# One core, linear attention into a two-layer network: the order of 4920 planned operations searched anew

## The chip, the cores and the metric

The program runs on one core of a Trainium2 chip. The metric is the device time of one execution in microseconds (us). TensorE multiplies matrices, VectorE, ScalarE and GpSimd (POOL) do the elementwise work, SP issues the DMAs. Each engine runs its own queue strictly in the order in which the program was written, and waits on semaphores for the others.

## The reference

```python
# attention: batch 8, heads 8, 576 tokens, head width 64, 128 random features
def phi(x):                                   # x already scaled by 64 ** -0.25
    h = einsum('bhsd,md->bhsm', x, omega) - sum(x * x, -1) / 2
    return exp(h - max(h, -1)) / sqrt(m)
kv, z = einsum('bhsm,bhsd->bhmd', phi(k), v), sum(phi(k), 2)
attn  = einsum('bhsm,bhmd->bhsd', phi(q), kv) / (einsum('bhsm,bhm->bhs', phi(q), z) + 1e-6)
# network over x = attn as 4608 tokens x 512
out = gelu(x @ w_in) @ w_out                  # w_in 512 x 2048, w_out 2048 x 512, gelu by erf
```

## The kernel before

The work is cut into operations of some 0.1 to 3 us: a Python function that issues a few instructions on one engine. There are 4920 of them. They are first recorded, each with what it reads and writes, and then issued one by one in the order of a table of numbers, ORDER, written out at the top of the file. The table sets the order of every engine's queue, SP's among them. A letter behind a number chooses one of three rings of PSUM banks. The loop that walks the table refuses an order in which an operation stands ahead of one that it depends on, and does nothing else:

```python
for x in ORDER.split():
    i = x.rstrip('abc')
    o, pick = self.ops[int(i)], x[len(i):] or 'a' * 4
    assert o.deps <= done and o.after <= done
    ...
    put(o)          # issues the operation's instructions
    done.add(o)
```

**Attention** is done in 32 units (u0 to u31), each two heads of one batch. Units 0 to 7 are plain (fp32): TensorE multiplies the features (pair, shared, L658, L665), VectorE takes the maximum of each tile (top, L670), ScalarE the exponential (exp_tiles, L674, in units 0 to 3; from unit 4 on VectorE shifts and one exps, L683, does the whole unit), TensorE sums keys by values (kv, L690), transposes the queries (q_trans, L728) and multiplies the two (num_plain, L738). Then ScalarE copies the denominator out (den), VectorE inverts it (rcp) and divides (div). Units 8 to 31 split operands in high and low parts. Their operations, as far as they are named below: x_high (ScalarE, L868) and x_low (POOL, L877) split the input, proj (TensorE, L885) and proj_q (L907) multiply the features, proj_add (VectorE, L895) adds and takes maxima, q_blocks (L910, L912), q_shift (L936), q_back (L943) and q_low (L949) on VectorE prepare the queries, k_shift (POOL, L903) shifts the keys, k_high (POOL, L408) and k_low (VectorE, L978) split them, kv_split (TensorE, L989) and kv_d (VectorE, L1010) form the sums, num (TensorE, L747) the result; v_max and v_b (VectorE, L1013, L970) scale the values.

**Weights.** 16 pieces are loaded (w_load, L475) and unpacked: w_hi (ScalarE, L480), w_shift (VectorE, L491), w_round (POOL, L497).

**The network** runs over 13 blocks of tokens: 256, 256, ten of 384, 256. In blocks 1 to 8, mm1(n,c) (TensorE, L1176) multiplies chunk c of the hidden layer in three parts of four matmuls into a PSUM bank of a ring of two, gelu and g_high (ScalarE, L1184, L1188) and g_low (VectorE, L1192) turn it into operands, and mm2 (TensorE, L1200 to L1202, three matmuls) multiplies by w_out. So mm1(n,c) can't begin before g_low(n,c-2) has left the bank. Block 0 runs in fp32 (L1171, L1197). Blocks 9 to 12 do the first product in seven products of half blocks (w_prod, L1389; w_mm2, L1487 to L1489; b_low and others); the sums of weights that they need are made by s_sum2 and s_sum (POOL, L1308 to L1317, L1301) and s_low (VectorE, L1327). An operation warm (TensorE, L434) multiplies zeros 22 times; nobody uses its result.

The order mixes all of this: while TensorE multiplies one block, the attention units of later batches pass through the other engines.

Of the kernel before, what the change touches and what calls it, by code (L numbers as in the profile page):

```python
# [34 lines left out]
0 3 6 7 151 42 41 157 4 1 8 43 9bca 14b 2 76 15 12 16 10 152 13 17 154 153 11 18 44aba 20 155 19 49b 45 21 47 50 51 163 77  # L35
156 52cc 158 27 55 22ba 48 160 53 159 5 54 161 56 31 46 23 29c 169 111 112 78 28 79cba 30 165 32 162 62 164 82 33cb 80 83
64b 166 57 34 167 81 35 65 36 84b 170 175 649 85 66b 113 58 114cba 86 172 63 171 119 115 87 117 116 173 120 90 121 37cc 24
59 67 25 91 60 92 88 181 650 38 89 39 177 176 68bb 40 93 122cc 69 178 118 70 97 179 652 98 71 168 99b 653 101b 72ba 26 123
100 187 651 685 94 655 102 127ba 125 656 182 654 73 184 657 183 103ab 74 124 185 658 75 104 659 126 105 193 188 189 132ba
128 660 106 174 190 136b 663 134 191 133 661 137 107bc 664 135 662 665 199 192 687 686 138cb 95 108 666 194 109 195 196  # L40
110 139 197 180 140 186 141 671 667 61 673 205 723 201 129 198 142bb 200 292 672 130 96 248 150 674 131 202 293 143 294
# [1581 lines left out]
```

## Time and profile before

| | |
|---|---|
| median of 3 runs | 970.92 us (970.18 to 971.43) |
| the profiled execution, first to last instruction | 968.7 us |
| TensorE busy | 945.4 us, 98% |
| VectorE busy | 768.5 us, 79% |
| ScalarE busy | 754.1 us, 78% |
| POOL busy | 416.9 us, 43% |
| mean granted clock of TensorE | 0.996 |
| moved by DMA | 71.0 MB, 73 GB/s |

The profile is of one execution; its span is 2.2 us below the median of the runs, which have some time around the first and last instruction. A busy TensorE is not one at its peak: the matmuls overlap, and each record lasts until its result is out. In the rows PE is TensorE, PEld its weight loads, DVE VectorE, ACT ScalarE; L12 is line 12 of the kernel before.

### The profile page before, as it was taken

How to read it: one execution, taken by the hardware profiler on the slowest of the kernel's cores; microseconds unless marked ns; L12 is line 12 of the kernel's file. 1: busy time of each engine (PE TensorE's matmuls, PEld its weight loads, DVE VectorE, ACT ScalarE, POOL GpSimd, SP SyncE). 2: the span in 40 equal slices, each digit the busy share in tenths (PEclk: the TensorE clock that was granted, in tenths of full speed). 3: DMA queues.
4: the chain of work that ended last, by engine and by line, in shares of the span. 5: the costliest groups of instructions: out<-in, count | busy, mean ns of one | idle time of the engine just before them, and what ended most of it. 6: DMA issues, size and time to landing. Idle time of an engine off the chain costs nothing.

```text
span 968.7 us, 18815 instructions
## 1 busy us (share of the span) xinstructions
PE 945.4 (98%) x6572; PEld 623.6 (64%) x6572; DVE 768.5 (79%) x2008; ACT 754.1 (78%) x1583; POOL 416.9 (43%) x620
## 2 busy tenths in 40 slices
PE   6989999999999999999999999999999999999998
PEld 5756666655556556566665666666657677677677
DVE  3889889999989988999997998999888764662322
ACT  6998688998798988988899788988887765664443
POOL 3464316784658526555553553542553302030000
PEclk9999999999999999999999999999999999999999
DMA  8985124421123123123222222221121000000000
GB/s 261 265 264 168 48 53 125 113 85 38 51 61 98 42 83 86 39 64 104 80 63 71 64 64 68 53 76 48 38 61 53 19 1 34 2 12 23 1 34 23
DMA packets 46286, 71.01 MB, mean 73 GB/s; under 512 B 13680, under 2 KB 22256, under 8 KB 46192
## 3 DMA queue, kind: packets, MB, share of 16 engines
q1 hardware_dynamic: 46192, 69.81, 25.0%
q8 instruction: 52, 0.85, 0.4%
q14 instruction: 42, 0.34, 0.1%
HBM read 60.36 MB, written 9.44 MB: 72 GB/s over the span
## 4 chain that ended last, share of the span: by engine, by line
PE 80%; DVE 10%; ACT 5%; issue 2%; DMA 2%; POOL 1%; SPq 0%; ACTq 0%; POOLq 0%; DVEq 0%
PE h L1176 20%; PE acc L1200 6%; PE acc L1201 6%; PE acc L1202 6%; PE at L1389 6%; PE h L1389 5%; PE acc L1487 4%; PE acc L1488 4%; PE acc L1489 4%; PE at L747 3%; PE acc L1197 3%; PE h L1171 3%; PE at L907 2%; PE at L885 2%; PE at L989 2%
## 5 line engine op out<-in xcount | busy, mean ns | idle before, releaser
L877 POOL TENSOR_TENSOR r<-xt,r 64x256 fp32r<-64x256 f32 (+2 forms) x216 | 176.9, 829 | 187.3 <-ACT r L868 160.1
L1176 PE MATMUL h<-xh,wih 128*128 128x384 f16 (+1 forms) x512 | 163.7, 320 | 4.2 <-DVE gl L1192 4.0
L1176 PE MATMUL h<-xh,wil 128*128 128x384 f16 (+1 forms) x512 | 163.7, 320 | 0.0
L1176 PE MATMUL h<-xl,wih 128*128 128x384 f16 (+1 forms) x512 | 163.7, 320 | 0.0
L1200 PE MATMUL acc<-woh,gh 128*128 128x512 f16 x368 | 140.4, 381 | 0.0
L1202 PE MATMUL acc<-wol,gh 128*128 128x512 f16 x368 | 139.5, 379 | 0.0
L1201 PE MATMUL acc<-woh,gl 128*128 128x512 f16 x368 | 139.4, 379 | 0.0
L1176 PEld LDWEIGHTS <-wih 128*128 128x128 f16 x1024 | 98.0, 98 | 61.0 <-issue 0.9
L868 ACT CAST r<-xt 128x256 fp32r<-128x256 f32 (+2 forms) x216 | 83.6, 404 | 17.1 <-PE at L907 9.8
L1192 DVE SCALAR_TENSOR_TENSOR gl<-h,bs,gh 128x384 f16<-128x384 f32 (+1 forms) x128 | 75.8, 592 | 10.1 <-ACT gh L1188 8.6
L1184 ACT ACTIVATE h<-h,bs 128x384 f32<-128x384 f32 (+1 forms) x128 | 69.1, 539 | 15.4 <-PE h L1176 14.5
L1188 ACT ACTIVATE gh<-h,bs 128x384 f16<-128x384 f32 (+1 forms) x128 | 72.3, 565 | 9.9 <-PE acc L1202 7.4
L1176 PEld LDWEIGHTS <-wil 128*128 128x128 f16 x512 | 50.0, 98 | 36.9 <-issue 7.2
L1487 PE MATMUL acc<-woh,gh 128*128 128x512 f16 (+1 forms) x192 | 69.5, 362 | 0.0
L1489 PE MATMUL acc<-wol,gh 128*128 128x512 f16 (+1 forms) x192 | 69.4, 361 | 0.0
L1488 PE MATMUL acc<-woh,gl 128*128 128x512 f16 (+1 forms) x192 | 69.4, 361 | 0.0
L1389 PEld LDWEIGHTS <-w 128*128 128x128 f16 x768 | 59.8, 98 | 7.0
L1202 PEld LDWEIGHTS <-gh 128*128 128x128 f16 x368 | 36.0, 98 | 43.4
L885 PE MATMUL at<-om,r 128*128 128x256 f32 x216 | 58.3, 351 | 1.3 <-DVE mx L918 0.7
L758 ACT ACTIVATE dt<-at,vsc 64x288 f32<-64x288 f32 x96 | 47.6, 496 | 10.7 <-PE at L747 8.4
L1200 PEld LDWEIGHTS <-gh 128*128 128x128 f16 x368 | 35.7, 97 | 28.5
L907 PE MATMUL at<-r,om 128*128 128x288 f32 x192 | 50.7, 355 | 1.1 <-POOL w L1308 0.6
(294 smaller groups left out, 2506.9 us busy)
## 6 DMA issues: line engine op xcount, KB each, us to landing
xt<-in_kT SPq DMA_DIRECT2D x56, 288.0 KB, 4.0
xt<-in_qT SPq DMA_DIRECT2D x56, 288.0 KB, 3.8
out_x<-o SPq DMA_DIRECT2D x35, 256.0 KB, 2.0
raw<-in_w_in SPq DMA_DIRECT2D x16, 512.0 KB, 5.2
raw<-in_w_out SPq DMA_DIRECT2D x16, 512.0 KB, 4.6
w<-in_v SPq DMA_DIRECT2D x24, 320.0 KB, 3.1
vt<-in_v SPq DMA_DIRECT2D x8, 320.0 KB, 6.3
out_x<-o SPq DMA_DIRECT2D x2, 128.0 KB, 1.7
```

Of the source, the lines that this page charges most:

```text
L868: nc.scalar.copy(G['r', u, x][:, 0:b - a], xf[:, a:b])
L877: nc.gpsimd.tensor_tensor(r, xf[D:, a:b], r, op=ALU.subtract)
L885: nc.tensor.matmul(o[:, t], r[:, t * P:(t + 1) * P], om, start=True, stop=True)
L1176: nc.tensor.matmul(h[:, 0:t], w, (G['xh', n, j], G['xh', n, j], G['xl', n, j])[k][:, 0:t], start=(i == 0), stop=(i == 3 * NJ - 1))
L1192: nc.vector.scalar_tensor_tensor(G['gl', n, c][:, 0:t], G['h', n, c][:, 0:t], G['bs', n][:, 3:4], G['gh', n, c][:, 0:t], op0=ALU.mult, op1 ...
L1200: nc.tensor.matmul(acc, gh[:, s], woh[:, c, c0:c1], start=(c == 0), stop=False)
L1201: nc.tensor.matmul(acc, gl[:, s], woh[:, c, c0:c1], start=False, stop=False)
L1202: nc.tensor.matmul(acc, gh[:, s], wol[:, c, c0:c1], start=False, stop=(c == NF - 1))
L1389: nc.tensor.matmul(b[:, g * h:(g + 1) * h], w, x[:, kt], start=first and k == 0, stop=last and k == 6 * GP - 1, skip_group_check=True)
L1487: nc.tensor.matmul(acc, gh, woh[:, c, c0:c1], start=begin, stop=False)
L1488: nc.tensor.matmul(acc, gl, woh[:, c, c0:c1], start=False, stop=False)
L1489: nc.tensor.matmul(acc, gh, wol[:, c, c0:c1], start=False, stop=end)
```

## The change

The table ORDER is replaced; nothing else in the file differs. The table is said to come from a new search, with durations read from a trace of these very operations. It has 190 lines for the old 196, so that every line of code below it has a number lower by 6. The first line of each:

```diff
 ORDER = """
-0 3 6 7 151 42 41 157 4 1 8 43 9bca 14b 2 76 15 12 16 10 152 13 17 154 153 11 18 44aba 20 155 19 49b 45 21 47 50 51 163 77
+0 3 4 6 9bca 1 10 7 11 14b 151 41 42 15 8 16 12 17bc 13 20 44aaa 152 153 49b 18 45 21 47 19 50 154 157 46 76 27ca 29c 31b 51
...
 """
```

Every engine issues as many instructions as before: TensorE 11194 with weight loads, VectorE 2010, ScalarE 1579, POOL 625, SP 217. Two places of the queues follow.

ScalarE's queue from its first instruction. et and w_71 are the exponentials of unit 0 and unit 1, raw is the raw weight piece, acc, h and at are PSUM banks. Before:

```order
L674 ACT_TABLE_LOAD
L674 ACTIVATE et<-acc,nm 128x128 x2
L480 ACTIVATE raw<-raw 128x1024
L674 ACTIVATE et<-h,nm 128x128 x4
L674 ACTIVATE et<-acc,nm 128x128 x4
L674 ACTIVATE et<-at,nm 128x128 x8
L674 ACTIVATE w_71<-acc,nm 128x128 x2
L504 ACTIVATE w_71,wmax<-w_71 128x1024
```

Now:

```order
L668 ACT_TABLE_LOAD
L668 ACTIVATE et<-acc,nm 128x128 x6
L668 ACTIVATE et<-h,nm 128x128 x4
L474 ACTIVATE raw<-raw 128x1024
L668 ACTIVATE et<-h,nm 128x128 x4
L668 ACTIVATE et<-acc,nm 128x128 x4
L668 ACTIVATE w_71<-at,nm 128x128 x4
L668 ACTIVATE w_71<-acc,nm 128x128 x2
```

Ten exponentials of unit 0 stand ahead of the first w_hi (raw) where two stood, and the first w_abs (L504) has gone further back.

VectorE's queue up to g_low(2,3), the gl in the last row but one before, for which the matmul mm1(2,5) waits. Rows of proj_add (ISA) are left out where they repeat. Before:

```order
L936 TENSOR_TENSOR w32_71<-w32_71,nq_2459 128x1152
L949 TENSOR_TENSOR ql_2505<-qt_2262,qh_2325 128x576
L1010 TENSOR_TENSOR kvl_2513<-kvz_2377,kvh_2497 128x256
L895 ISA et_82,nm_2371<-at_2492,lo_2503 128x128
...
L970 SCALAR_TENSOR_TENSOR vb_1266<-w32_71,vsc_1798,vb_1266 128x10x64
L1327 SCALAR_TENSOR_TENSOR w32_71<-w32_71,wsc_80 128x256
L910 STREAM_TRANSPOSE et_82<-at_2526 128x288
L912 TENSOR_REDUCE mx_2527<-et_82 128x9
L943 STREAM_TRANSPOSE qt_2551<-w32_71 128x576
L1192 SCALAR_TENSOR_TENSOR gl_2559<-h_2402,bs_1464,gh_2546 128x384
L978 TENSOR_TENSOR vt_73<-w32_71,vt_73 128x256 x2
```

Now (g_low(2,3) is the gl of the fourth row):

```order
L889 ISA et_82,nm_2351<-at_2435,lo_2456 128x128
L1321 SCALAR_TENSOR_TENSOR w32_71<-xa_83,wsc_80,w32_71 128x256
L964 SCALAR_TENSOR_TENSOR vb_1246<-w32_71,vsc_1802,vb_1246 128x10x64
L1186 SCALAR_TENSOR_TENSOR gl_2517<-h_2413,bs_1464,gh_2499 128x384
L889 ISA et_82,nm_2351<-at_2439,lo_2491 128x128
...
L943 TENSOR_TENSOR ql_2521<-qt_2367,qh_2424 128x576
L1004 TENSOR_TENSOR kvl_2531<-kvz_2374,kvh_2495 128x256
L930 TENSOR_TENSOR w32_71<-w32_71,nq_2404 128x1152
L904 STREAM_TRANSPOSE et_82<-at_2503 128x288
L906 TENSOR_REDUCE mx_2504<-et_82 128x9
```

The q_shift (w32_71 with nq), both q_low (ql), kv_d (kvl) and the q_blocks stand behind g_low where they stood ahead of it.

## Rows read from the trace of the kernel before

**Rows 1.** The page, part 1: busy time, share of the span, instructions.
```profile
PE 945.4 (98%) x6572; PEld 623.6 (64%) x6572; DVE 768.5 (79%) x2008; ACT 754.1 (78%) x1583; POOL 416.9 (43%) x620
```
**Rows 2.** Busy time by stretch: from:to, length, each engine's us, clock, DMA share, GB/s.
```profile
0.00:75.00 75.00, 62.66 (x497) 46.34 (x498) 51.83 (x134) 62.61 (x148) 36.73 (x36) 0.95 0.86 259
160.00:320.00 160.00, 154.97 (x977) 96.89 (x976) 150.98 (x410) 140.50 (x305) 108.00 (x163) 1.00 0.24 68
725.00:969.00 244.00, 240.39 (x2108) 176.52 (x2105) 121.54 (x272) 138.66 (x281) 37.06 (x62) 1.00 0.06 20
```
**Rows 3.** TensorE's waits, 75 to 960 us: who for whom, total us, times, longest.
```profile
PE h L1176 <- DVE gl L1192: 4.0, 7, 1.3
PE at L989 <- DVE vt L978: 1.0, 1, 1.0
PE at L885 <- DVE mx L918: 0.7, 1, 0.7
PE at L885 <- POOL r L877: 0.6, 1, 0.6
PE at L907 <- POOL w L1308: 0.6, 1, 0.6
PE at L907 <- DVE nm L895: 0.6, 1, 0.6
PE h L1176 <- DVE vexp L1030: 0.2, 1, 0.2
```
**Rows 4.** Timeline of TensorE at a wait: start, us, line, tiles; idle before in brackets.
```profile
217.10 0.38 PE L1201 MATMUL acc<-woh,gl 128*128 128x512 f16 x1
217.31 0.38 PE L1202 MATMUL acc<-wol,gh 128*128 128x512 f16 x1
218.98 0.32 PE L1176 MATMUL h<-xh,wih 128*128 128x384 f16 x1 [1.29 <-DVE gl L1192]
```
**Rows 5.** Timeline of the start: VectorE's maxima, ScalarE, TensorE.
```profile
8.70 0.68 DVE L670 TENSOR_REDUCE nm<-h 128x4 f32<-128x512 f32 x1
...
8.82 0.63 ACT L674 ACTIVATE et<-acc,nm 128x128 f32<-128x128 f32 x2 [6.81 <-DVE nm L670]
10.75 1.17 ACT L480 ACTIVATE raw<-raw 128x1024 f32<-128x1024 f32 x1 [1.30 <-DMA raw<-in_w_in]
11.81 1.13 ACT L674 ACTIVATE et<-h,nm 128x128 f32<-128x128 f32 x4
...
5.19 0.55 PE L658 MATMUL acc<-om,xt 64*128 64x128 f32 x1 [5.19 <-DMA xt<-in_kT]
6.85 0.42 PE L658 MATMUL h<-om,xt 64*128 64x128 f32 x1
8.24 3.39 PE L434 MATMUL h<-w 128*128 128x256 bf16 x22
```
**Rows 6.** Busy time by 5 us (columns as in rows 2), 15 to 25 us.
```profile
15.00:20.00 5.00, 3.27 (x29) 2.67 (x25) 2.54 (x6) 5.00 (x15) 0.14 (x1) 1.00 0.98 237
20.00:25.00 5.00, 3.27 (x21) 2.71 (x22) 0.84 (x5) 5.00 (x17) 3.46 (x2) 0.52 1.02 335
```
**Rows 7.** Groups by line: total us, mean ns of one, idle before.
```profile
L936 DVE TENSOR_TENSOR w<-w,nq 128x1152 f32<-128x1152 f32 x11 | 15.2, 1380 | 2.2 <-POOL nq L930 1.7
L949 DVE TENSOR_TENSOR ql<-qt,qh 128x576 fp32r<-128x576 f32 x48 | 40.2, 838 | 0.4 <-ACT qh L946 0.2
L1327 DVE SCALAR_TENSOR_TENSOR w<-w,wsc 128x256 f16<-128x256 f32 x18 | 12.9, 721 | 0.0
L903 POOL TENSOR_TENSOR et<-et,nm 128x1152 f32<-128x1152 f32 x13 | 28.6, 2197 | 7.5 <-DVE nm L895 7.3
```
**Rows 8.** Timelines of VectorE and POOL ahead of that wait.
```profile
214.53 2.33 DVE L1327 SCALAR_TENSOR_TENSOR w<-w,wsc 128x256 f16<-128x256 f32 x1
213.95 2.62 POOL L903 TENSOR_TENSOR et<-et,nm 128x1152 f32<-128x1152 f32 x1 [1.06 <-DVE nm L895]
```
**Rows 9.** Timeline of TensorE at the last num_plain(u2,1).
```profile
51.10 0.66 PE L738 MATMUL h<-qh,kvz 128*64 128x288 f32 x4
```

More of the change, by code (lines that the diff above doesn't have):

```diff
@@ L34 @@
 ORDER = """
-0 3 6 7 151 42 41 157 4 1 8 43 9bca 14b 2 76 15 12 16 10 152 13 17 154 153 11 18 44aba 20 155 19 49b 45 21 47 50 51 163 77
-156 52cc 158 27 55 22ba 48 160 53 159 5 54 161 56 31 46 23 29c 169 111 112 78 28 79cba 30 165 32 162 62 164 82 33cb 80 83
-64b 166 57 34 167 81 35 65 36 84b 170 175 649 85 66b 113 58 114cba 86 172 63 171 119 115 87 117 116 173 120 90 121 37cc 24
-59 67 25 91 60 92 88 181 650 38 89 39 177 176 68bb 40 93 122cc 69 178 118 70 97 179 652 98 71 168 99b 653 101b 72ba 26 123
@@ L39 @@
-100 187 651 685 94 655 102 127ba 125 656 182 654 73 184 657 183 103ab 74 124 185 658 75 104 659 126 105 193 188 189 132ba
-128 660 106 174 190 136b 663 134 191 133 661 137 107bc 664 135 662 665 199 192 687 686 138cb 95 108 666 194 109 195 196
-110 139 197 180 140 186 141 671 667 61 673 205 723 201 129 198 142bb 200 292 672 130 96 248 150 674 131 202 293 143 294
[153 rows of a table removed]
-4423 4372 3470 3887 3468 4424 4373 4371 4434 3471 3469 4438 4374 4369 3891 3472 4435 4425 3889 4432 4439 4375 3892b 4492
-4433 4442 4491 4376 3894 4377 3893 4378 3896 4379 3895 4436 3900 4497 4437 3897 4498 3905 4451 3901 3898 3909 4452 3906
@@ L197 @@
-4293 3899 3907 4038 3473 4385 3910 3474 4382 3908 3902 4440 3475 4502 4441 4300 3903 4388 3911 3913b 3904 4301 3912 3476
[4 rows of a table removed]
-4466 3977 4467 3978 4468 4395 4469 4479 4470 3979 4396 3950b 4471 4397 3952 4477 3951 3980 4480 3953 3954 4478 4398 3958
-3955 3956 3963 4472 3959 3957 3981 3964 4481 4482 3965 4473 3960 3966 3982 4542 3967 3961 4543 4006 4483 4503 4007 4474
-3962 3968 3983b 4475 3969 4008 3970 4045 4009 3984 4010 3985 3987 3986 3989 3988 3993 4011 3994 4012 4046 3995 4013 4047
-4484 4049 4014 3990 4015 4485 3991 4016 3992 4494 4017 4048 4507 3998 4050 4508 3996 4051 4018 3999 4052 4002 4053 4054
@@ L206 @@
-4057b 4003 3997 4004 4019 4000 4005 4020 4058 4001 4021 4495 4496 4022 4023 4059 4024 4055 4025 4061 4056 4026 4027 4499
-4028 4500 4060 4029 4062 4063 4067 4064 4065 4504 4068 4032 4512 4066 4513 4069 4033 4517 4072 4070 4505 4071 4076 4030
-4589 4501 4073 4031 4506 4080 4518 4077 4078 4103 4074 4079 4104 4034 4075 4509 4519 4081 4035 4105 4510 4521 4514 4106
-4511 4525 4520 4529 4107 4526 4082b 4522 4084 4083 4530 4515 4086 4085 4516 4090 4533 4087 4088 4523 4091 4527 4095 4092
-4528 4108 4089 4096 4109 4524 4097 4099 4098 4486 4100 4531 4110 4487 4532 4111 4488 4112 4534 4113 4489 4114 4138 4093
@@ L211 @@
-4535 4139 4101 4094 4115b 4536 4537 4102 4538 4117b 4116 4539 4540 4140 4118 4119 4541 4141 4120 4121 4142 4143 4122 4125
-4567 4544 4546 4545 4130 4548 4126 4552 4568 4550 4570 4144 4131 4547 4145 4571 4551 4569 4554 4127 4146 4549 4123 4555
-4147 4553 4132 4124 4556 4148 4557 4149 4134 4128 4558 4150 4559 4135 4560 4129 4173 4136 4561 4174 4137 4562 4133 4175
-4564 4151 4563 4176 4565 4573 4566 4581 4582 4152b 4572 4583 4574 4177 4584 4585 4586 4154 4153 4575 4178 4753 4587 4593
-4576 4156 4588 4155 4179 4157 4577 4180 4578 4160 4158 4579 4181 4165 4161 4580 4182 4166 4169 4167 4159 4162 4590 4183
@@ L216 @@
-4168 4170 4184 4591 4594 4185 4163 4592 4186 4754 4164 4171 4607b 4755 4595 4172 4597 4187 4596 4599 4598 4188 4756 4601
-4600 4189 4757 4603 4602 4605 4190 4608 4604 4758 4609b 4606 4611 4610 4759 4191 4613 4612 4192 4193 4614 4194 4615 4195
-4760 4617 4196 4618 4622 4616 4197 4198 4626 4623 4630b 4632 4631 4627 4199 4633 4200 4619 4634 4201 4620 4202 4636 4635
-4621 4640 4637 4638 4645 4641 4761 4653 4646 4649 4628 4647 4629 4654 4624 4639 4665b 4648 4625 4655 4666 4667b 4656 4668
-4669 4650 4671 4670 4675 4672 4642 4657 4676 4658 4659 4680 4684 4660 4661 4662 4663 4664 4688 4643 4689 4685 4644 4673
@@ L221 @@
-4700 4651 4674 4690 4652 4701 4691 4681 4692 4677 4693 4694 4695 4702b 4696 4703 4704 4697 4705 4698 4699 4706 4678 4679
-4710 4707 4708 4723 4711 4686 4715 4709 4682 4687 4724 4683 4725 4719 4726 4720 4727 4716 4717 4728 4762 4729 4712 4763
-4730 4764 4718 4766 4731 4765 4768 4767 4732 4769 4774b 4733 4734 4776b 4713 4735 4721 4714 4736 4777 4722 4737 4775 4738
-4778 4780 4779 4739 4781 4770 4740 4772 4771 4743 4741 4773 4744 4782 4745 4783 4746 4784 4789 4785 4786 4749 4747 4793
-4748 4742 4750 4794 4797 4787 4790 4799b 4788 4798 4820 4795 4800 4796 4801 4791 4821 4792 4751 4802 4803 4752 4807 4804
@@ L226 @@
-4805 4822 4808 4806 4823 4809 4824 4825 4826 4827 4828 4829 4830 4812 4831 4816 4810 4813 4855 4811 4817 4832b 4818 4814
-4819 4856 4815 4833 4857 4858 4859 4834b 4860 4835 4861 4862 4863 4836 4864 4837 4838 4842 4839 4840 4847 4843 4841 4844
-4865 4851 4848 4867 4866 4868 4890 4852 4869b 4871 4870 4845 4891 4872 4853 4846 4873 4849 4854 4877 4850 4874 4875 4892
-4878 4876 4882 4879 4886 4883 4893 4887 4884 4894 4895 4885 4896 4897 4898 4899 4900 4901 4902 4880 4888 4903 4881 4889
-4904 4905 4908 4906 4909 4910 4911 4907 4912 4913 4914 4917 4915 4916 4918 4919
+0 3 4 6 9bca 1 10 7 11 14b 151 41 42 15 8 16 12 17bc 13 20 44aaa 152 153 49b 18 45 21 47 19 50 154 157 46 76 27ca 29c 31b 51
@@ new lines @@
+48 43 22ba 52ab 23 53 77 28 32 79baa 158 155 57ca 30 159 160 54 55 84c 56 24 80 161 156 85 62ba 163 64b 111 169 162 58 164
+112 33ac 86 65 82 166 81 34 25 165 35 36 63 83 66a 59 114bba 119a 67 26 171 78 87aa 115 117 170 167 37cc 120 116 172 68bb 121
+90 38 173 175 649 88 91 176 60 650 39 40 61 181 69 113 92aa 178 89 122cc 93 70 123 97aa 652 71 118 177 655 98 124 99b 653 100
+656 179 101a 654 102 125 187 651 182 72bb 73 103cb 184 74 657 183 126 658 75 686 127aa 659 132ca 136b 104 105 168 188 133 106
@@ new lines @@
+134b 185 137 660 107bc 2 663 135 661 94 662 664 108 174 665 190 193 128 109 129 685 110 194 95 189 130 138bb 721 671 139 191
+96 131 192 196 140 195 673 666 672 674 180 688 186 146 141 199 292 293 142bb 200 197 294 296 295 198 205 297 667 689 723 248
[146 rows of a table added]
+3465 3466 3459 4430 4419 4291 3460 3463 4434 3874 3470 4424 3471 3472 3890a 3467 4368 4428 4361 4435 3883 4431 4425 3867 4292
+4438 4420 4429 3468 3875 4432 3884 3469 4433 3885 4289 3886 3888 3887 4490 4436 3473 3474 3891 3475 3892b 4039 4371 3894 4437
@@ new lines @@
+3893 4439 4366 4369 4492 4290 4442 3476 4491 4364 3895 4440 4441 3896 3897 3900 4443 3901 4298 4365 4444 3905 4367 3477 3889
+4497 3906 3902 3479 3478 4299 4372 4373 4445 3898 4374 3899 3907 4375 4376 4377 3482 3903 3909 4378 4446 3908 3936 3937 3910
+3904 4447 3480 3871 4451 4300 4448 4379 3911 3938 3913b 3939 4036 4301 3912 3914 3915a 4302 3940 3483 4382 3917 3919 3941
+4449 4303 3916 4304 3942 4450 3920 4457 4293 4388 3918 4452 3923 4383 3943 4458 3944 3945 3946 4386 4461 4040 4453 4455 3947
@@ new lines @@
+3924 3921 4462 4305 4380 3925 3922 4306 3926 3928 4307 4387 4389 3971 4459 3932 3972 3948a 3927 3933 3934 4460 4456 4381 4454
+3973 3935 4391 3974 4463 4037 4464 4390 4465 3975 4466 3929 3930 4493 4392 3931 4393 4394 4467 4468 4469 4043 3976 4470 4476
+3977 3978 4479 4395 3979 4044 3950b 3980 4396 3981 4397 4477 3949 3952 4471 3982 3951 4398 4041 3954 4478 4498 3953 4472 3955
+3958 4482 3959 3956 4502 3963 3960 3967 3961 3957 4006 3962 4007 4008 4009 3964 3968 3965 3966 3969 3983b 3970 4010 3984
@@ new lines @@
+3985a 3987 4045 4384 4483 3989 4042 4473 4011 4012 4013 4484 3986 4014 4485 3481 4015 3988 4494 3993 3994 3998 4046 3990 4503
+4002 4047 4016 4048 4507 3999 3991 4000 4057b 4003 3992 4017 4495 3995 4001 4058 4508 4474 4059a 3996 4496 3997 4049 4018
+4019 4050 4060 3484 4004 4005 4020 4051 4061 4499 4504 4021 4022 4480 4023 4062 4500 4063 4053 4064 4024 4055 4065 4026 4512
+4052 4054 4067 4072 4513 4073 4517 4056 4027 4028 4029 4032 4518 4033 4066 4068 4481 4505 4501 4030 4069 4074 4076 4070 4077
@@ new lines @@
+4103 4506 4078 4071 4025 4104 4034 4075 4079 4080a 4509 4510 4081 4519 4514 4511 4105 4521 4106 4107 4082b 4083 4525 4084
+4108 4109 4086 4522 4085 4526 4090 4095 4087 4110 4088 4515 4529 4096 4089 4520 4111 4091 4112 4097 4516 4092 4527 4098 4528
+4523 4099 4113 4114 4093 4524 4542 4530 4531 4533 4100 4486 4532 4589 4138 4534 4115b 4094 4535 4536 4101 4102 4537 4543 4538
+4116 4117a 4487 4539 4540 4541 4139 4140 4544 4141 4142 4488 4119 4118 4546 4120 4143 4144 4121 4145 4146 4545 4567 4568 4125
@@ new lines @@
+4475 4489 4122 4570 4147 4123 4148 4547 4130 4548 4554 4126 4149 4124 4127 4031 4550 4555 4134 4128 4135 4549 4571 4131 4552
+4556 4136 4173 4553 4569 4551 4174 4557 4558 4129 4175 4137 4150a 4176 4132 4559 4560 4133 4177 4178 4561 4562 4563 4564 4151
+4573 4565 4572 4574 4566 4152b 4581 4582 4179 4583 4154 4575 4576 4153 4156 4584 4157 4577 4155 4160 4180 4578 4181 4585 4158
+4579 4161 4586 4182 4183 4580 4587 4593 4162 4184 4165 4169 4595 4159 4590 4163 4597 4164 4594 4166 4167 4599 4168 4596 4170
@@ new lines @@
+4171 4185 4598 4591 4753 4601 4186 4187 4188 4038 4603 4607b 4172 4189 4609b 4592 4600 4190 4610 4608 4602 4193 4611 4612
+4605 4194 4604 4613 4617 4614 4606 4035 4754 4615 4622 4191 4195 4196 4616 4618 4199 4760 4200 4619 4620 4626 4623 4630b 4653
+4756 4197 4757 4627 4621 4631 4654 4632a 4633 4192 4634 4636 4635 4640 4624 4201 4628 4625 4629 4655 4656 4657 4658 4641 4659
+4645 4660 4649 4650 4661 4646 4662 4637 4665b 4638 4642 4639 4663 4647 4664 4643 4666 4667b 4688 4669 4668 4670 4758 4644
@@ new lines @@
+4671 4648 4759 4689 4672 4755 4690 4651 4652 4675 4676 4691 4680 4692 4693 4684 4677 4202 4694 4695 4696 4673 4697 4700a 4698
+4674 4685 4699 4723 4724 4678 4702b 4701 4679 4762 4764 4686 4681 4725 4703 4198 4704 4726 4687 4682 4706 4705 4588 4707 4727
+4728 4729 4730 4761 4710 4683 4711 4715 4719 4731 4732 4708 4709 4766 4733 4720 4763 4765 4712 4734 4735 4713 4721 4767 4714
+4774b 4776b 4716 4722 4736 4717 4768 4737 4718 4769 4738 4739 4775 4770 4740 4743 4744 4778 4772 4771 4741 4777 4779 4773
@@ new lines @@
+4745 4780 4784 4789 4785 4746 4781 4747 4782 4793 4749 4742 4783 4790 4797a 4750 4799b 4820 4798 4786 4787 4821 4801 4794
+4800 4795 4788 4796 4791 4822 4803 4751 4823 4824 4804 4825 4805 4802 4826 4807 4792 4827 4828 4808 4806 4812 4829 4830 4809
+4813 4831 4855 4810 4811 4816 4832b 4817 4818 4856 4819 4834b 4752 4857 4833 4814 4836 4858 4835 4859 4860 4838 4861 4839
+4837 4815 4842 4840 4862 4863 4843 4864 4847 4851 4852 4844 4865 4841 4867a 4866 4845 4869b 4868 4846 4890 4871 4891 4848
+4853 4854 4873 4870 4892 4872 4893 4877 4878 4894 4849 4874 4895 4896 4882 4875 4879 4850 4886 4897 4898 4899 4900 4883 4876
@@ L231 @@
+4901 4887 4902 4884 4880 4888 4903 4881 4889 4885 4904 4905 4908 4748 4906 4907 4909 4910 4911 4912 4913 4914 4917 4915 4916
+4918 4919
 """
```

303 rows, old and new, of the table ORDER are left out of this document.

## The prediction

> **What bounds the kernel now.** I read the page first, then the busy time by stretches, the waits of TensorE, and the single rows behind them. TensorE is busy for 945.4 of 968.7 us and VectorE for 768.5 [rows 1]. The operations are fixed, so all that an order can win is TensorE's idle time, 23.3 us, or 2.4%. The stretches say where it lies [rows 2]: 75.00 - 62.66 = 12.3 us before 75 us, 5.0 from 160 to 320, and 3.6 after 725, which is the last stores behind the last matmul (0.3 of it lies beyond the span). The next engine is VectorE: from 160 to 320 us it is busy for 151.0 of 160, but after 725 only for 121.5 of 244 [rows 2]. So VectorE's place in the queue decides there, and work that can wait until 725 us is free.
>
> After 75 us TensorE waited 13 times, 7.7 us in all, and 5.0 of these for VectorE's L1192 (g_low) and L978 (k_low) [rows 3]. The idle time is not the whole delay: the matmul at 218.98 starts 1.67 us after the one at 217.31, where that one started 0.21 after its own predecessor. So 1.46 us are lost and 1.29 are shown [rows 4]. I add 0.17 us to each wait.
>
> In the first 75 us ScalarE leads. Its first exponential starts at 8.82 us; later it stands for 1.30 us until the raw weights have landed at 10.75 [rows 5]; and from 15 to 25 us it is busy without a pause [rows 6].
>
> **The change, part by part.** All engines have the same number of instructions in both orders, and ScalarE the same 56 table loads. Nothing is added or removed, so only waits can change.
>
> *Start.* Before, ScalarE runs two exponentials, then w_hi of the first piece, then four, four and eight. Now ten exponentials (pa, shared and pb tiles of unit 0) stand ahead of w_hi, and VectorE takes the pa tile's maximum first. I take that tile to be ready when the second of the pair matmuls ends, at 6.85 + 0.42 = 7.27 us. With 0.68 us for the maximum, the price of the one at 8.70, the first exponential can start at 7.95, which is 0.87 earlier. At 1.13 us for four, ten take 2.8 us and end at 10.8, when the weights are there. So the wait of 1.30 us is filled too, and the sum is 0.87 + 1.30 = 2.17 us [rows 5]. Behind them ScalarE has the same work up to the exponentials of unit 4, so I let it keep these. The bounds: nothing, if another engine's chain sets the pace further on; 12.3 - 5.2 = 7.1 us, if all of TensorE's idle time goes but that before the first input has landed [rows 2, 5]. I stay at 2.17, since ScalarE is the full engine in the rows that follow [rows 6].
>
> SP's queue moves too: k comes ahead of q for unit 1, and v of unit 0 ahead of the second weight piece. That piece lands later by one load, and with it its w_hi and w_round; kv of unit 0 gets its v earlier. I count neither, since the exponentials cover both; without that cover they lie between the same two bounds, 0 and 7.1 us, or cost the time of one load.
>
> *VectorE's queue at the waits.* At seven of the 13 places I compared what stands ahead of the awaited instruction in both orders.
>
> - mm1(2,5), 218.98 us, idle 1.29: eleven VectorE operations go behind g_low(2,3), and none comes ahead of it. One q_shift (1.38 us), two q_low (0.84 each) and an s_low (0.72) alone make 3.8 us [rows 7]; kv_d, two v_max, q_back, q_blocks and two proj_add come on top. TensorE loses two operations ahead of mm1: an mm2, 3 x 0.21 = 0.63 us [rows 4], and a num, which I price by a row of the plain kind, 0.66 [rows 9]. The lead grows by at least 3.8 - 1.3 = 2.5 us.
> - kv_split(u28,4), idle 1.0 [rows 3]: TensorE has twelve more operations ahead of it. Nine are mm1 or mm2; at the 0.63 us of an mm2 they make 5.7 us. VectorE has three fewer ahead of the k_low.
> - The other five are mm1 operations that waited for g_low: (1,10), (3,2), (3,8), (5,1), (8,13). Ahead of g_low 5, 6, 10, 10 and 3 VectorE operations leave, and 2, 0, 1, 0 and 1 join. At (3,2) g_low had itself waited for ScalarE's g_high; there six operations leave too, and none joins.
>
> At the first two the lead grows by more than the wait; at the others, most of which lose as many operations, I take the same, since no wait is longer than 1.3 us [rows 3]. So I count the waits for L1192 and L978 as gone: 5.0 us shown in eight waits, and 8 x 0.17 = 1.36 us not shown, together 6.36 us. What is late next are the units whose operations were put back. The other five waits (2.7 us, [rows 3]) I leave, as a stand-in for new ones. Bounds: nothing, if new waits as large appear elsewhere; 7.7 + 13 x 0.17 = 9.9 us, if all go.
>
> *POOL.* The eight s_sum2, one block before, are now spread over a stretch of the program that is several times as long. This may free POOL where proj_q waited for one of them, 0.6 us [rows 3]. I count nothing: POOL is busy for 108 of 160 us there [rows 2], so other work of its own can take that place. The bounds lie within those of the waits.
>
> *End.* The last TensorE operations are the same, so the 3.6 us stay.
>
> **A rule against the change.** The largest wait stands behind a stretched VectorE instruction. L1327 at 214.53 took 2.33 us, where its kind takes 0.72 on average; it ran while POOL's L903, of 2.62 us, was under way, and ended within 0.3 us of its end [rows 7, 8]. The Trainium skill, SBUF — State Buffer, section "Who interferes with whom", has a reason: VectorE and GpSimd share a port pair that one of them holds for a whole instruction while the other is blocked. The trace agrees. By that rule the durations in a trace belong in part to the old neighbours, a search that uses them plans for stalls that are no longer there, and the later term would be 0 in place of 6.36 us.
>
> **Sum.** -2.17 - 6.36 = -8.5 us: a span of 960.2 us against 968.7. The median of the runs is 970.9, 2.2 above the span, so 962.4 us, 0.9% less.
>
> **The rivals.**
>
> *Nothing is left to wait for.* All 9.9 us after 75 us go, and 7.1 at the start: 970.9 - 17.0 = 953.9 us. For it speaks that more operations left than joined at all seven places; against it, that durations vary from run to run and that the start hangs on a chain through four engines. Chance 0.12.
>
> *The stretched instructions move.* Each of the units 8 to 31 has a k_shift on POOL, 2.2 us (L903), and where one met a VectorE instruction with two inputs, 2.33 - 0.72 = 1.6 us were lost [rows 7, 8]. With new neighbours, new waits as large as the old come up elsewhere: 970.9 - 2.2 = 968.7 us. Against it: VectorE now has more lead at the places looked at, which would swallow one such loss. Chance 0.22.
>
> *A cold clock, and slower.* The 22 warm-up matmuls (L434) stood third in TensorE's queue at 8.24 us [rows 5]. Now they stand behind num_plain(u2,1), and nothing fills the gaps ahead of it. The granted clock was 0.52 in 20 to 25 us, the lower of the two levels, after TensorE had been busy for 3.27 of 5 us in 15 to 20 [rows 6]. In the old order num_plain(u2,1) ends at 51.10 + 0.66 = 51.8 us [rows 9], 46.6 after the first matmul. Take off the warm-up, 3.4 us, and the idle time, 7.1 us at most [rows 2, 5], and 36.1 us are work; so 10.5 us are slack. A stretch at 1.2 GHz loses half of its length: 21 us of it cost nothing, and from 2 x (10.5 + 8.5) = 38 us on it eats the whole gain. At that level throughout, the work ends at 5.2 + 72.2 = 77.4 us, 25.6 late, and the rest keeps its 6.4: 970.9 - 6.4 + 25.6 = 990.1 us. For it: the start now has gaps and no filler. Against it: the first four operations need only loads, and in all of the first 75 us the mean was 0.95 [rows 2]. Chance 0.08. The Trainium skill, TensorE: Matmul & The Clock Gate, section "What's actually happening", says that the slow level is the default and that activity lifts it; rows 6 agree for the fall.
>
> That the change does nothing can't be: the queues differ from the second row on.
>
> **How the numbers follow.** The forecast has 0.58, with a range of its own from 957.5 to 966.5 us, the stand-in of 2.7 us and the larger part of the head's bounds to either side. The range is 955 to 970 us: it takes in the forecast, most of the stretched case and the edge of the first rival, and leaves out the clock case. No change is within 0.2%, 1.9 us, about what a measurement here can tell: 969.0 to 972.8. Faster: 0.58 + 0.12 + half of the stretched case, 0.81. No change: 0.10, from its other half. Slower: 0.09, the clock and a little of the stretched case.
>
> **What would show it.** Right: the first L668 exponential near 8 us, with ten ahead of w_hi and no wait for raw; TensorE's waits after 75 us at 3 us or less, hardly any of them for L1186 or L972; TensorE's idle time before 75 us near 10 us. Wrong: waits for L1186 as large as before at other places, with VectorE instructions of 2 us ahead of them; a granted clock near 0.5 over more than 25 us; or an idle time before 75 us of 12 us or more.

## The result and the profile after

The changed kernel takes 980.62 us (median; 979.92 to 980.85) against 970.89 us for the kernel before, measured beside it. The ratio is 1.0102, with a 95% interval of 1.0087 to 1.0116: about 1% slower, 9.7 us, where 8.5 us less were forecast. The lines of code have numbers lower by 6 in this kernel: L1186 is the old L1192 (g_low), L972 the old L978 (k_low), L897 the old L903 (k_shift).

First the page's busy time, then the stretches, with the columns of [rows 2].

```profile
PE 948.1 (97%) x6572; PEld 622.8 (64%) x6572; DVE 766.2 (78%) x2008; ACT 748.1 (76%) x1583; POOL 415.5 (42%) x620
```

```profile
0.00:75.00 75.00, 65.77 (x522) 50.08 (x523) 51.90 (x133) 63.88 (x150) 35.04 (x31) 0.95 0.87 261
160.00:320.00 160.00, 152.69 (x962) 95.07 (x960) 146.97 (x403) 135.45 (x296) 97.18 (x147) 1.00 0.24 64
```

No engine has more to do than before [rows 1]. Ahead of 75 us TensorE is idle for 75.00 - 65.77 = 9.2 us where it was 12.3 [rows 2], so the start is better, and its clock is the same 0.95. From 160 to 320 us the idle time rose from 5.0 to 7.3 us, although VectorE is less busy there.

The waits of TensorE from 75 us on, who for whom, total, times and longest, answer to [rows 3]:

```profile
PE at L983 <- DVE vt L972: 3.7, 4, 1.8
PE at L879 <- DVE nm L889: 2.8, 2, 1.5
PE at L732 <- DVE et L673: 2.1, 2, 1.3
PE at L901 <- ACT kvz L998: 1.5, 1, 1.5
PE h L1383 <- DVE at L1396: 1.5, 1, 1.5
PE at L901 <- POOL vt L402: 1.4, 1, 1.4
PE at L741 <- ACT kvz L998: 1.2, 1, 1.2
PE h L1170 <- DVE gl L1186: 1.1, 3, 0.4
...
PE acc L1195 <- DVE cm L1011: 0.2, 1, 0.2
```

With five lines that are left out here they make 18.0 us, where [rows 3] make 7.7. The waits for g_low fell from 4.0 to 1.1 us, as forecast. But kv_split (L983) now waits 3.7 us for k_low, and num_plain (L732), proj (L879), proj_q (L901) and w_prod (L1383) wait where none or less was before.

What stands ahead of the new waits? Here are three of them: for each VectorE's instruction, the one of POOL beside it, and TensorE's wait that follows (start, duration, line, tiles; idle time before in brackets). First kv_split(u12,2) behind k_low(u12,2):

```profile
291.81 2.33 DVE L972 TENSOR_TENSOR vt<-w,vt 128x256 f16<-128x256 f32 x1
291.69 2.17 POOL L897 TENSOR_TENSOR et<-et,nm 128x1152 f32<-128x1152 f32 x1
294.20 0.26 PE L983 MATMUL at<-vb,vt 128*128 128x65 f16 x2 [1.78 <-DVE vt L972]
```

Then a product of block 9 that waits for c_sum, some instructions behind b_low(9,4), L1352:

```profile
744.37 2.55 DVE L1352 SCALAR_TENSOR_TENSOR xl<-w,bs,xh 128x384 f16<-128x384 f32 x1
744.39 2.11 POOL L897 TENSOR_TENSOR w<-w,nm 128x1152 f32<-128x1152 f32 x1
749.86 0.24 PE L1383 MATMUL h<-xh,w 128*128 128x192 f16 x1 [1.50 <-DVE at L1396]
```

And num_plain behind split_om, L439, which splits the random features once; here POOL's instruction is w_round (L491), not k_shift:

```profile
100.14 2.53 DVE L439 TENSOR_TENSOR om<-om,om 128x128 fp32r<-128x128 f32 x1
100.12 2.40 POOL L491 TENSOR_TENSOR w<-w,raw 128x1024 int32<-128x1024 int32 x1 [4.47 <-DVE om L438]
105.66 0.46 PE L732 MATMUL at<-qh,kvz 128*64 128x288 f32 x2 [1.34 <-DVE et L673]
```

Each time VectorE's instruction starts beside a long one of POOL and ends within half a us of it: 2.3 to 2.6 us for work that takes 0.4 to 0.6 elsewhere. That is the pattern of [rows 8], at other places.

To see how much there is of it I took each kind of VectorE's instruction by itself (same line, operation and shape), from 60 us on. The duration that a quarter of them stay under stands for undisturbed, and I summed what the others take beyond it. In the kernel before, 1105 instructions overlap one of POOL and lose 53.4 us, and 800 don't and lose 3.7; after, it is 53.2 us for 1109 and 4.2 for 794. The sums hang on the mark that is chosen (with the duration that only a tenth stay under, it is 59.8 and 57.6 us beside POOL), but by neither mark do they rise. **So the sum did not grow. What changed is where it falls.** Five instructions lost more than 1.3 us before, nine after, k_low(u12,2) and b_low(9,4) among them. (split_om stands alone in its kind and loses nothing by this count.)

### The profile page after: what moved, and what is told of

It is laid out like the page before. It is cut to its first block, busy times and chain, and to the rows that moved or that the text cites. A ratio compares the mean times of both kernels' runs of the same rounds, so it can differ in the third digit from the quotient of the medians.

```text
span 979.1 us, 18778 instructions
## 1 busy us (share of the span) xinstructions
PE 948.1 (97%) x6572; PEld 622.8 (64%) x6572; DVE 766.2 (78%) x2008; ACT 748.1 (76%) x1583; POOL 415.5 (42%) x620
## 4 chain that ended last, share of the span: by engine, by line
PE 69%; DVE 16%; ACT 11%; issue 3%; DMA 0%; POOL 0%; SPq 0%; ACTq 0%; DVEq 0%
PE h L1170 16%; PE acc L1194 5%; PE at L1383 5%; PE acc L1195 5%; PE acc L1196 5%; PE h L1383 5%; PE acc L1481 4%; PE acc L1483 4%; PE acc L1482 4%; PE at L741 3%; PE h L1165 2%; PE acc L1191 2%; PE at L879 2%; DVE vt L972 2%; PE at L901 2%
## 5 line engine op out<-in xcount | busy, mean ns | idle before, releaser
L871 POOL TENSOR_TENSOR r<-xt,r 64x288 fp32r<-64x288 f32 (+2 forms) x216 | 170.1, 799 | 207.4 <-ACT r L862 170.3
L862 ACT CAST r<-xt 128x256 fp32r<-128x256 f32 (+2 forms) x216 | 83.9, 405 | 16.9 <-PE at L901 8.8
L1186 DVE SCALAR_TENSOR_TENSOR gl<-h,bs,gh 128x384 f16<-128x384 f32 (+1 forms) x128 | 76.0, 593 | 21.4 <-ACT gh L1182 20.4
L1383 PEld LDWEIGHTS <-w 128*128 128x128 f16 x768 | 60.2, 98 | 11.2 <-issue 2.5
L1195 PEld LDWEIGHTS <-gl 128*128 128x128 f16 x368 | 36.1, 98 | 25.5 <-DVE gl L1186 1.0
L883 ACT COPY lo<-at 128x256 f32<-128x256 f32 (+1 forms) x120 | 40.9, 350 | 13.9 <-PE at L879 11.0
```

What stands on the lines that cost most here:

```text
L862: nc.scalar.copy(G['r', u, x][:, 0:b - a], xf[:, a:b])
L871: nc.gpsimd.tensor_tensor(r, xf[D:, a:b], r, op=ALU.subtract)
L1186: nc.vector.scalar_tensor_tensor(G['gl', n, c][:, 0:t], G['h', n, c][:, 0:t], G['bs', n][:, 3:4], G['gh', n, c][:, 0:t], op0=ALU.mult, op1 ...
L1195: nc.tensor.matmul(acc, gl[:, s], woh[:, c, c0:c1], start=False, stop=False)
L1383: nc.tensor.matmul(b[:, g * h:(g + 1) * h], w, x[:, kt], start=first and k == 0, stop=last and k == 6 * GP - 1, skip_group_check=True)
```

## The experiments

The theory: POOL's long instructions (k_shift, 2.1 us; w_round, 2.4) hold up VectorE's instructions with two SBUF inputs, and the new order puts other instructions beside them. (That the search went wrong because it planned with the durations of the old neighbourhood is an argument; no run here tests the search.) The main rival: the new queues are too tight by themselves. A second one: the loss is a late consequence of the new start.

**1. Start and rest apart.** The two tables have nearly the same operations in their first 270 places (7 differ). One kernel takes the first 270 from the new table and all others in the old order; the other the reverse. The first edit, in short:

```diff
-ORDER = after
+ORDER = after[:270] + [x for x in before if x not in after[:270]]
```

> The first 270 places of the changed table (to about 68 us), then all other operations in the old order. Theory 'the head is better, the loss comes later': the trace of the change reaches place 270 some 1.7 us earlier than the old one (68.2 against 70.0 us), so about 969 us. Rival 'the new head leaves the later stages worse placed, and the loss is its consequence': above 975 us.

Measured: 968.67 us against 970.54 beside it, ratio 0.998 (0.997 to 0.9989).

> The reverse: the first 270 places of the old table, then all other operations in the changed order. Theory 'the loss comes later': 980.6 + 1.7, about 982 us. Rival 'the loss is a consequence of the new head': near 971 us.

Measured: 983.84 us, ratio 1.0139 (1.0124 to 1.0154). So the new start is worth 1.9 us ahead of the old rest (970.54 - 968.67) and 3.2 ahead of the changed one (983.84 - 980.62), and the loss lies in the rest alone: it is there, and larger, behind the old start.

**2. k_shift cut to one of nine tiles**, in both orders.

```diff
-        nc.gpsimd.tensor_tensor(es, es, G['nm', u][:, 0:NT].unsqueeze(2)...
+        nc.gpsimd.tensor_tensor(u.et[:, 0:1], u.et[:, 0:1], G['nm', u][:, 0:1].unsqueeze(2)...
```

> The changed kernel, with k_shift done on the first of its nine tiles of 128 columns only, so the other eight are not shifted; POOL's instruction of 2.1 us becomes one of some 0.3 us, the queues stay as they are. Theory 'POOL's long k_shift stretches VectorE's two-input instructions, and the new order puts k_low, kv_d, b_low, s_low beside it where TensorE waits for them': eight of TensorE's waits after 200 us stand behind such a stretched instruction, some 13 us; 8 to 13 us go, 968 to 973 us, and no k_low or b_low of over 1.3 us is left. Rival 'the new queues are too tight by themselves, whatever the neighbours': the waits stay, 978 to 980 us.

Measured: 969.03 us, ratio to the kernel before 0.9982 (0.9972 to 0.9991).

> The kernel before with the same cut in k_shift. Theory 'neighbours': only the waits at 219 and 716 us stand behind a stretch by k_shift, 2 to 3 us with what follows them, so 967 to 969 us, and the gap between the two orders, 9.7 us, shrinks to under 5. Rival 'too tight by itself': a gain as large or as small as in the changed order, and the gap stays at 8 to 11 us.

Measured: 966.95 us, ratio 0.9965 (0.9952 to 0.9978). The changed order gains 11.6 us by the cut and the old one 3.6 (against 970.54). The gap of 9.7 us becomes 2.1. The waits of TensorE after 75 us in the changed order with the cut, the three largest of 7.9 us, where it was 18.0 without the cut:

```profile
PE at L732 <- DVE et L673: 2.1, 2, 1.3
PE at L879 <- DVE nm L889: 0.9, 1, 0.9
PE at L983 <- DVE vt L972: 0.8, 2, 0.6
```

Where k_low(u12,2) had lost 1.9 us, the same piece of VectorE's queue now reads (q_back, three k_low together, the next g_low):

```profile
287.72 0.77 DVE L937 STREAM_TRANSPOSE qt<-w 128x576 f32<-128x576 f32 x1
288.42 2.21 DVE L972 TENSOR_TENSOR vt<-w,vt 128x256 f16<-128x256 f32 x3
290.56 0.60 DVE L1186 SCALAR_TENSOR_TENSOR gl<-h,bs,gh 128x384 f16<-128x384 f32 x1
```

In the changed kernel these three k_low take 3.92 us:

```profile
290.22 3.92 DVE L972 TENSOR_TENSOR vt<-w,vt 128x256 f16<-128x256 f32 x3
```

The longest k_low or b_low now takes 1.15 us, under the 1.3 of the expectation, and of the nine instructions that lost over 1.3 us one is left, w_low(1,1), which w_round stretches (experiment 4). The queues are the same in both, so "too tight by itself" falls as the main cause. But the cut also makes the chain from the maxima through k_shift to the exponential shorter, which the next experiment takes away.

**3. k_shift in three instructions**, all of its work done, in both orders.

```diff
-        nc.gpsimd.tensor_tensor(es, es, G['nm', u][:, 0:NT].unsqueeze(2)...
+        for t in range(0, NT, 3):
+            nc.gpsimd.tensor_tensor(es[:, t:t + 3], es[:, t:t + 3], G['nm', u][:, t:t + 3].unsqueeze(2)...
```

> The changed kernel with k_shift issued as three instructions of three tiles each; all work is done, the chain through k_shift is no shorter. Theory 'VectorE is blocked for the whole of one POOL instruction': no instruction loses more than some 0.7 us at a time, so no k_low or b_low of over 1.3 us is left, and of the 11.6 us that the cut to one tile gave about half or more comes back, 970 to 975 us. Rival 'the cut helped because the chain maxima, k_shift, exponential became 1.8 us shorter': nothing is gained, 979 to 982 us.

Measured: 973.73 us, ratio 1.0028 (1.0019 to 1.0037).

> The kernel before with the same three instructions. Theory 'blocked for a whole instruction': the waits at 219 and 716 us shrink, 967 to 970 us. Rival 'shorter chain': no gain or a small loss, 970 to 972 us.

Measured: 969.68 us, ratio 0.9984 (0.9974 to 0.9993). With no less work for POOL and no shorter chain the changed order wins back 6.9 of the 11.6 us, against 1.1 in the old order. The longest k_low or b_low in it takes 1.25 us, and again only w_low(1,1) loses over 1.3. POOL's groups (total us, mean ns of one) and the three k_low at the same place, in the changed order:

```profile
L898 POOL TENSOR_TENSOR et<-et,nm 128x384 f32<-128x384 f32 x39 | 33.9, 895 | 0.6
...
L898 POOL TENSOR_TENSOR w<-w,nm 128x384 f32<-128x384 f32 x33 | 30.5, 950 | 1.6 <-DVE nm L889 1.0
```

```profile
288.34 2.63 DVE L973 TENSOR_TENSOR vt<-w,vt 128x256 f16<-128x256 f32 x3
```

POOL's total for k_shift rose from 52.0 to 64.4 us. Most of that is the price of more instructions: the median piece takes 0.83 us, and a third of the whole one (median 2.11) would be 0.70, which makes some 9 us for 72 pieces. The rest are longer pieces, up to 1.83 us; that POOL waits for VectorE there is likely, but not shown. Whether the other 4.7 us of the cut come from what the shorter instructions still block or from the shorter chain, these runs don't separate.

**4. w_round cut as well**, to 128 of its 1024 columns, beside the cut of experiment 2, in both orders.

```diff
-        nc.gpsimd.tensor_tensor(pc.b, pc.b, pc.l or raw(pc)[1], op=ALU.add)
+        nc.gpsimd.tensor_tensor(pc.b[:, 0:128], pc.b[:, 0:128], (pc.l or raw(pc)[1])[:, 0:128], op=ALU.add)
```

> The changed kernel with k_shift cut to one tile and w_round (POOL, 2.4 us) cut to the first 128 of its 1024 columns, so that the weights of the rest are not rounded. In the changed order w_round stretches w_low(1,1) by 2.1 us at 73 us and split_om by 2.2 us at 100 us, and TensorE waits 0.8 and 1.3 us for exps behind them. Theory 'neighbours': these two waits go, 2 to 3 us less than with k_shift alone, 966 to 967 us. Rival 'they are waits of the order itself': 969 us, as with k_shift alone.

Measured: 966.08 us, ratio 0.9944 (0.9929 to 0.9959). Both waits of num_plain for L673 are gone, and split_om takes 0.59 us where it took 2.53:

```profile
98.81 0.59 DVE L439 TENSOR_TENSOR om<-om,om 128x128 fp32r<-128x128 f32 x1
```

> The kernel before with k_shift cut to one tile and w_round cut to 128 of 1024 columns, beside the changed order with the same cuts, 966.1 us. In the old order TensorE does not wait between 75 and 160 us, so theory 'neighbours' expects next to nothing from w_round: 965.5 to 967.5 us, and the two orders within 1 us of each other, where they were 9.7 apart. A rival, that a shorter w_round helps by itself in any order: 964 us or less.

Measured: 966.10 us, ratio 0.995 (0.9937 to 0.9962). Here are the pairs together:

| | old order | changed order | gap |
|---|---|---|---|
| as they are | 970.89 | 980.62 | +9.7 |
| k_shift in three | 969.68 | 973.73 | +4.1 |
| k_shift cut to one tile | 966.95 | 969.03 | +2.1 |
| w_round cut too | 966.10 | 966.08 | 0.0 |

The whole gap goes with POOL's two long instructions; for w_round, as for k_shift, the cut takes away work and shortens a chain too, and no run cuts w_round in pieces. What stays open: the new start is worth 1.9 us, so with both cuts the changed order should lead by as much. Something of that size is left in its later part, and no run here says whether it is the shorter instructions of POOL or the queues.

**5. The order alone, again.** In the changed table three k_shift go one step back in POOL's queue, each behind the x_low that followed it. Each number stands for one operation; the lines between stay.

```diff
-1840 1896
+1896 1840
...
-2566 2957 2563
+2957 2563 2566
...
-3724 2880 3808
+2880 3808 3724
```

> The changed table with three numbers moved and no other edit: k_shift(u13), k_shift(u19) and k_shift(u26) each go behind the x_low that followed them in POOL's queue. Theory 'neighbours': k_low(u12,2), k_low(u18,2) and v_b(u25) lose under 1 us each in place of 1.92, 1.93 and 1.48; the waits of 1.78 us at 294 and of 1.37 at 442 go for the most part, 2.5 to 4.5 us in all, 976 to 978 us. Rival 'the queues are too tight by themselves': VectorE's and TensorE's queues are the same, so the waits stay, 980 us or more.

Measured: 979.08 us, ratio 1.0082 (1.0069 to 1.0096): 1.5 us less than the changed kernel, not 2.5 to 4.5, and below the rival's 980 as well. The moves did what they were made for, and the trace shows why that isn't enough. The three k_low at 290 us take 2.01 us together in place of 3.92, and the wait of 1.78 us is gone, but the k_shift that was moved meets the next two-input instruction in VectorE's queue, an s_low (L1322 here), and behind it stands a new wait:

```profile
290.59 2.01 DVE L973 TENSOR_TENSOR vt<-w,vt 128x256 f16<-128x256 f32 x3
...
293.91 1.94 DVE L1322 SCALAR_TENSOR_TENSOR w<-w,wsc 128x256 f16<-128x256 f32 x1
```

```profile
293.46 2.11 POOL L898 TENSOR_TENSOR et<-et,nm 128x1152 f32<-128x1152 f32 x1
```

```profile
296.64 0.23 PE L984 MATMUL at<-vb,vt 128*128 128x130 f16 x1 [1.00 <-DVE vt L973]
```

The third k_shift that was moved no longer stretches v_b(u25), but a q_shift, which now takes 2.95 us. The wait of proj_q at 442 us is gone without a successor.

**6. Towards a version that beats both.** The kernel of experiment 1 with the new start, then two k_shift moved in its later part, then k_shift in three; all the work is done in each.

```diff
-1290 472 1698 1277 845 834 846 1233 843 847 1212 835 1278 1213 1149 848 1214
+472 1698 1277 845 834 846 1233 843 847 1212 835 1278 1213 1149 848 1214 1290
...
-4351 3426 4346 4411 4298 3439 4350 4283 3427 3440 4280 4352 4284 4296 3434 3432 4353 4412
+3426 4346 4411 4298 3439 4350 4283 3427 3440 4280 4352 4284 4296 3434 3432 4353 4412 4351
```

> The first 270 places of the changed table, the rest in the old order, and k_shift in three instructions: a correct kernel that joins the two gains. If they add, 968.7 less the gain of three instructions in the old order (1 to 3 us), 965.5 to 967.5 us; if the waits that k_shift caused are replaced by others, 968 us or more.

Measured: 967.27 us, ratio 0.9957 (0.994 to 0.9974), in the range.

> The first 270 places of the changed table, the rest in the old order, and two numbers moved in it: k_shift(u11) behind k_high(u10,2) and k_shift(u29) behind x_low(u30,2). Theory 'neighbours': s_low(5,0) and k_low(u28,3) are no longer stretched by 1.9 us and the waits of 1.3 and 1.0 us behind them go; 968.7 less 2 to 3 us, 965.5 to 967 us. Rival: the moved k_shift stretches others that TensorE waits for, 968 us or more.

Measured: 967.24 us, ratio 0.9963 (0.9951 to 0.9976): 1.4 us better than without the moves, a little less than expected, and between the theory's range and the rival's. Again one wait has a successor: s_low(5,0) takes 0.47 us, but two k_low behind it now take 2.99 together, and mm1 at that place waits 1.07 us where it had waited 1.29.

```profile
211.59 0.47 DVE L1321 SCALAR_TENSOR_TENSOR w<-w,wsc 128x256 f16<-128x256 f32 x1
...
214.19 2.99 DVE L972 TENSOR_TENSOR vt<-w,vt 128x256 f16<-128x256 f32 x2
```

> The same table with k_shift in three instructions: 964.5 to 967 us if the two means add a little, 967 us or more if the moves bring nothing once no instruction of POOL is longer than 0.8 us there.

Measured: 965.13 us (964.4 to 966.41), ratio 0.9943 (0.9931 to 0.9955): 0.6% below the kernel before and some 15 us below the changed one. It has the lowest median of all kernels here that do the whole work, but its interval overlaps those of the other two of this experiment, so that their order among themselves isn't shown.

## Why the prediction was wrong

**The start: right.** The forecast for ScalarE was 7.95 us for the first exponential, ten of them ahead of w_hi, no wait for the raw weights, and 2.17 us. ScalarE's queue (a row can join several instructions):

```profile
8.04 1.66 ACT L668 ACTIVATE et<-acc,nm 128x128 f32<-128x128 f32 x6 [6.02 <-DVE nm L664]
9.55 1.18 ACT L668 ACTIVATE et<-h,nm 128x128 f32<-128x128 f32 x4
10.77 1.16 ACT L474 ACTIVATE raw<-raw 128x1024 f32<-128x1024 f32 x1
```

The exponential started at 8.04, w_hi at 10.77 with no wait before it, and experiment 1 measured 1.9 us ahead of the old rest. TensorE's idle time before 75 us is 9.2, where "near 10" was the sign for it.

**The cold clock: fell.** The warm-up starts at 48.72 us, and the last num_plain(u2,1) ahead of it ends at 48.13 + 0.66 = 48.8 us, 3.0 earlier than [rows 9]:

```profile
48.13 0.66 PE L732 MATMUL h<-qh,kvz 128*64 128x288 f32 x4
```

The mean granted clock of the first 75 us is 0.95 in both kernels, so the case of a cold clock did not come.

**The waits named: right, as far as they go.** None of the eight waits that were counted as gone is left at its place. (For one of them, that of mm1(4,11), the lead had not been looked at.) Of the other five two are back at the same operations: proj(u13,2) waits 0.8 us where it waited 0.7, and proj_q(u12,1) 1.5 where it waited 0.6. But the sign for it was "hardly any" wait for L1186 or L972, and the two make 1.1 + 3.7 = 4.8 us again, where it was 5.0, now at other operations.

**The step that failed** is the one behind that: "The other five waits (2.7 us) I leave, as a stand-in for new ones", with the bound "nothing, if new waits as large appear elsewhere". The new waits are 18.0 - 1.1 = 16.9 us, not 2.7, and so the term was not -6.36 us but a loss: 18.0 - 7.7 = 10.3 us more are shown idle after 75 us. The prediction's 0.17 us for each wait fits: 21 waits in place of 13 make 1.4 us more, 11.7 together, and the rest of the table lost 9.7 + 1.9 = 11.6. I looked only at the places where the old order waited, and two of these, at 219 and 716 us, stood behind an instruction that chance had stretched. That other neighbours are better there says nothing of the places where the new order would be hit. And the bound below nothing was left out without a reason for it, though the same text had a row of 2.33 us for an operation of 0.72 [rows 7, 8].

**The rival that was right in kind** is "The stretched instructions move", at 0.22. It held that the new neighbours bring waits as large as the old. The total loss of VectorE beside POOL did stay (53.4 and 53.2 us), but TensorE's waits are no fixed share of that total: 18.0 us of them stand against 7.7. They go with the few instructions that lose over 1.3 us, five before and nine after, though not one to one: with k_shift cut, eight of the nine are gone and 10.1 of the 18.0 us. So its price had no ceiling at "no gain".

**The rule** of the Trainium skill, SBUF — State Buffer, section "Who interferes with whom", was cited against the term and then outweighed by a lead that was counted in mean durations. It says that the port pair is an exclusive lock, and that a VectorE instruction with two inputs in SBUF contends for it with a GpSimd instruction that reads SBUF, while one with at most one such input does not, outside of certain modes. The trace agrees. Counted by operation from 60 us on, in the changed kernel 59 k_low that overlap POOL lose 14.6 us and the other 61 lose 0.2; 85 g_low overlap POOL too, one of their two tiles (h) lies in PSUM, and they lose 0.5 us in all. The longest k_low takes 2.34 us beside a whole k_shift, the longest g_low 0.62. So the mechanism that the prediction gave a chance of its own made most of the loss: 6.9 of the 11.6 us went with the pieces of experiment 3 alone.

## What to carry to other kernels

A duration read from a trace can belong to its neighbours as much as to its instruction: one k_low took 0.4 us, another 2.3. Before an order is planned with such numbers, split each kind into its undisturbed time and the time beside the engine that can block it, and charge the second by what the new order puts beside it. Where a long instruction can hold up a full engine, try to cut it in pieces before reordering around it: here that took 6.9 us from the order that had been hit and 1.1 from the other, while moving it by hand mostly moved the wait. When forecasting a new order, look for what will be hit in it, not only at the old waits. (Whether the old order was lucky or the new one unlucky, two tables can't tell.)

## What the runs showed that was not expected

- How sharply the kinds part. Counted in the same way, in the kernel before 94 g_low, 85 q_blocks, 72 proj_add, 39 rcp and 33 q_back overlap an instruction of POOL, and together they lose 2.7 us; 71 k_low, 23 s_low and 13 kv_d lose 13.5, 6.4 and 3.2.
- ScalarE shows nothing of the kind: after 75 us its instructions lose 0.1 us in all beyond the usual spread of their kinds (durations more than 15% over the median), in either order.
- What pieces cost: as three instructions k_shift takes POOL 64.4 us where it took 52.0 as one, most of it some 0.12 us for each piece, and the kernel was 6.9 us faster all the same.
- How local the effect of an order is: behind place 270 nearly every operation has moved, half of them by 15 places of the table or fewer; that gives 9.7 us of difference, and none once two of POOL's instructions are cut short.
